# Routing ranks and loads reordered in the prologue, a ramp issued early, and MoE buffers placed above the attention output

## The chip, the cores and the metric

The kernel runs on one core of a Trainium2 chip. The metric is the device time of one execution in microseconds. Before the change it is 383.17 us, the median of 3 runs (382.03 to 384.43). The profiled execution has a span of 377.3 us; all times inside the kernel below are counted from the start of that span.

## The reference

The computation has two parts. The first is attention with a relative-position bias, for 8 batches, 8 heads, 576 positions and head size 64:

```
scores = q @ k^T / sqrt(64) + bias_table[bucket(|i - j|)]     per head
x      = softmax(scores) @ v            -> reshaped to [8*576, 512]
```

The bucket depends on the distance alone; distances of 128 and more share the last bucket. The second part is a mixture of experts (MoE) with a hashed choice: token t goes to expert `token_ids[t] * 2654435761 % 8`, and its row becomes `relu(x @ w1[e]) @ w2[e]`, with w1 of 512 x 1024 and w2 of 1024 x 512 for each of 8 experts. Since the multiplier is odd and ends in binary 001, the expert is the low three bits of the token's id.

## The kernel before

**Attention.** The 8 batches and 4 head pairs give 32 pairs, handled one after the other by a loop over n (0 to 31), with one more turn (n = 32) that finishes the last pair. For one pair:

- `load` and `load_v` bring q, k and v in; `cast_q` (L274) and `cast_k` (L283) on VectorE make 16-bit copies qh and kh; `cast_v` (L289) does so on ScalarE into vt.
- `transpose_q` and `transpose_k` transpose on TensorE (L457, L472) into a PSUM buffer of the tag aux, which has two buffers, and VectorE copies the result to qt (L465) and to kz (L478, L479). There are three kz; half of each is zero for good, written once by `z_init`.
- `scores(n, g)` for g = 0 to 3 multiplies into one of two PSUM buffers of the tag ps (L502), and ScalarE takes the exponential into att: three large ones (L513) and a tail (L507).
- `band` multiplies the exponentials near the diagonal by the exponential of the bias, ebd, on VectorE (L532). The last rows use ebd in two pieces for the first four pairs (L547), and later ebs, one piece (L552), which `make_ebs` copies from ebd. `low_bands` is the part of the bands that needs the tail.
- `av_steps(n)` is a generator: `advance(av, k)` issues the next k matmuls of att against v (L579) into two aux buffers in turn, with a reciprocal and a product (L589, L590) after each, which write the rows of x_all. It runs one pair behind: turn n holds the av of pair n - 1.

**Order.** [...] it is written out by hand. [...] Loads from HBM stand in SyncE's queue (`nc.sync`), some in ScalarE's and GpSimd's.

**Bias.** The table is loaded as tbl, turned by a small matmul (L712) and an exponential (L718) into one row per head, written to HBM (t_f, L722) and read back shifted by partition with `load_bias` (L727) into ebd.

**Routing.** `route` is a generator of twelve steps: te (low bits of the ids raw), tef (16-bit copy), ef (transposed by TensorE, L312), oh (one-hot), then the ranks inc and rnk (two matmuls into a ps buffer, L338 and L339, a scan and a subtraction), mx, flag and so on to the slot numbers ds2. Steps are taken in the prologue, at n = 0 and from n = 3 on. From n = 14 on, `name_slot` (L619) writes each token's row number to its slot in HBM by an indirect DMA from GpSimd; all slots are then loaded back as xid.

**The seam.** `store` (L634, L639) writes x_all to HBM. `gather(e, ...)` (L153) fetches five blocks of 128 rows for expert e by indirect DMAs from GpSimd; for expert 0 this happens at n = 30, when all batches but one are stored. The rows of the last batch that belong to expert 0's first block are fetched by a matmul with a one-hot matrix instead: `hot_slots` is a generator whose first step writes a ramp on GpSimd (L404) and a copy of the slots on VectorE (L408), and whose later steps make one matrix hot each (L414). `first_rows` (L424, L428) transposes blocks 1 to 4 inside turn 31, `first_slots` (L443, L448) makes block 0.

**MoE.** For each expert, 64 matmuls make hps (L953) in two PSUM buffers, ScalarE makes h from it (L959), 40 matmuls make ops (L977), VectorE copies them to ok (L984), and GpSimd scatters the rows to the output (L985). The pool of the MoE buffers (h1, xpt, ok) opens when attention's pool closes, and takes the same addresses: h1 lay where x_all had been.

Of the kernel before, what the change touches and what calls it, by code (L numbers as in the profile page):

```python
# [31 lines left out]
def kernel(  # L32
# [160 lines left out]
    with tc.tile_pool(name="at", bufs=1) as at, tc.tile_pool(  # L193
# [52 lines left out]

        def load_v(n):
            b, m = pairs[n]
            for hh in range(2):
                nc.sync.dma_start(  # L250
                    out=vf[n % 4][:, hh, :, :],
                    in_=v[b, 2 * m + hh, :NB4].rearrange(
                        "(t p) d -> p t d", p=P
                    ),
                )
# [262 lines left out]
        def band(n, g, lo=0):  # L518
# [20 lines left out]
            else:  # L539
                a = att[:, NU - 1, :QW].rearrange("p (o u) -> p o u", o=2)[  # L540
                    :, :, :EW
                ]
                if n < NPAIR:
                    for hh in range(2):
                        w0 = EW - HD * hh
                        r = slice(D * hh, D * hh + D)
                        nc.vector.tensor_tensor(  # L547
                            out=a[r], in0=a[r],
                            in1=ebd[r, :, m, hh, w0 : w0 + EW], op=ALU.mult,
                        )  # L550
                else:
                    nc.vector.tensor_tensor(  # L552
                        out=a, in0=a, in1=ebs[:, :, m, :], op=ALU.mult
                    )
# [88 lines left out]
        def advance(it, count):  # L643
            for _ in range(count):
                if next(it, "end") == "end":
                    return
# [11 lines left out]
        ohsb = at.tile([2 * NB, FW], F16, name="ohsb")  # L658
        nc.scalar.dma_start(out=ohsb[:, :], in_=OH_d.ap())
        nc.gpsimd.dma_start(out=ident[:, :], in_=I128_d.ap())  # L660
        load(0, "qk")
        load(1, "qk")

        def z_init(i):
            nc.vector.memset(kz[i][D:P, :S].bitcast(I32), 0)
            nc.vector.memset(kz[i][:D, S:].bitcast(I32), 0)

# [40 lines left out]
        z_init(1)  # L708
        z_init(2)
        FH = FW // 2  # L710
        for i in range(2):
# [11 lines left out]
            out=F_d.ap(), in_=ebsb[:, :, :].rearrange("h a b -> h (a b)")  # L723
        )
        def load_bias(eng, m0, m1, b2):
            for o in range(2):
# [11 lines left out]
        def make_ebs():  # L738
            for hh in range(2):
# [7 lines left out]
                )  # L747

        cast_q(0)
        cast_k(0)  # L750
        v_init(0)
        vs_init(0)
        for i in range(1, 4):
            v_init(i)
        nobody = at.tile([P, NSLOT // P, 2], I32, name="nobody")
        nc.gpsimd.memset(nobody[:, :, :], BIG)
        load_bias(nc.scalar, 0, 1, 0)
        load_bias(nc.sync, 0, 1, 1)
        load(0, "v")
        load(2, "qk")  # L760
        load_vs(0, nc.gpsimd)
        ids = moe_token_ids.bitcast(I32).rearrange(
            "(b s c) -> b s c", b=B, c=2
        )
        nc.gpsimd.dma_start(out=raw[:1, :, :], in_=ids[B - 1 :])
        nc.gpsimd.dma_start(out=raw[1:, :, :], in_=ids[: B - 1])
        nc.gpsimd.dma_start(out=msk[:, :], in_=MSK_d.ap())
        nc.gpsimd.dma_start(out=cnt[:, :], in_=CNT_d.ap())
        transpose_q(0)
        keep_busy(idp[:, :], 1)  # L770
        transpose_k(0)
        keep_busy(idp[:, :], 1)
        cast_q(1)
        cast_k(1)
        routing = route()
        advance(routing, 2)
        nc.gpsimd.tensor_copy(out=pace[:, :], in_=kh[1][:1, 0, 0, 0:1])
# [27 lines left out]
        for n in range(NP + 1):  # L805
# [11 lines left out]
            if n == 1:  # L817
                vs_init(1)
            if n == 3:
                make_ebs()  # L820
# [15 lines left out]
            for g in range(NSG + 1):  # L836
                scores(n, g)
                if 3 <= n < 14 and g == 1:
                    next(routing, None)
# [4 lines left out]
                if n == NP - 1:  # L844
                    for sc in ((), (1,), (2, 3), (4,))[g]:
                        first_rows(sc)
                if NP - 2 <= n and g in (0, 1, 3):
                    next(hotting, None)
                if n == 0:
                    if g == 1:  # L850
                        transpose_q(1)
                        transpose_k(1)
                        advance(routing, 2)
                        band(n, 0)
# [8 lines left out]
                elif n == 1:  # L863
# [4 lines left out]
                    elif g == 1:  # L868
                        advance(av, 27)
                        band(n, 0)  # L870
                    elif g == 2:
                        advance(av, 99)
                        band(n, 1)
                        band(n, 2)
                    elif g == 3:
                        transpose_k(2)
                        transpose_q(2)
                        cast_v(1)
# [5 lines left out]
                elif g == 0:  # L884
                    if n < NP - 1:
                        transpose_k(n + 1)
                    low_bands(n - 1)
                    advance(av, 12)
                elif g == 1:
                    if n == 2:  # L890
                        transpose_q(3)
                        cast_v(2)
                        load_v(6)
                        cast_q(4)
                    if n + 2 < NP:
                        cast_k(n + 2)
                    if 2 < n < NP - 1:
                        cast_v(n + 1)
                    advance(av, 15)
                    band(n, 0)  # L900
                elif g == 2:
                    if n < NP - 3:
                        cast_q(n + 3)
                    if n == 2:
                        cast_v(3)
                    advance(av, 99)
# [12 lines left out]
    with tc.tile_pool(name="mo", bufs=1) as mo, tc.tile_pool(  # L919
        name="mop", bufs=1, space=bass.MemoryType.PSUM  # L920
    ) as mop:
        NRC = 2
        NR = CAP // NRC
# [208 lines left out]
```

The softmax here doesn't subtract the row's maximum and nothing guards it: scores larger than these inputs give would overflow.

## Time and profile before

| engine | busy us | share of 377.3 us |
|---|---|---|
| TensorE matmul | 329.2 | 87% |
| ScalarE | 237.2 | 63% |
| VectorE | 218.7 | 58% |
| GpSimd | 186.3 | 49% |

| stretch, us | VectorE busy | ScalarE busy | TensorE matmul busy | granted TensorE clock |
|---|---|---|---|---|
| 8 to 20 | 9.67 | 9.26 | 9.79 | 1.00 |
| 20 to 30 | 8.28 | 5.23 | 7.20 | 0.83 |
| 140 to 160 | 19.04 | 17.92 | 17.67 | 1.00 |
| 190 to 200 | 4.68 | 6.45 | 9.61 | 0.72 |
| 200 to 210 | 2.98 | 4.36 | 3.17 | 0.79 |
| 210 to 222 | 7.96 | 3.55 | 9.96 | 0.89 |
| 242 to 260.5 | 3.52 | 8.51 | 18.50 | 1.00 |

A share of the whole span mixes three stages with different limits, so the second table is of more use: in steady attention (140 to 160) VectorE and ScalarE are both nearly full, in the MoE (242 to 260.5) TensorE alone is. Between 190 and 222 us no engine is full. Rows of one operation can overlap by about 0.1 us, so that a busy sum can come near the length of its stretch with short gaps left.

The tail exponentials (L507), one for each pair, are a clock of the attention's progress: pair 0 at 14.82, 1 at 20.05, 2 at 31.29, 3 at 38.36, 4 at 44.93, 13 at 98.37, 28 at 186.14, 29 at 195.89, 30 at 202.26, 31 at 216.18. The first full h of the MoE starts at 224.54.

### The profile page before, as it was taken

Reading aid. Unit: us, or ns where it says so; the run is one execution under the profiler, and the core shown is the slowest. Engines: PE = TensorE matmul, PEld = TensorE weight load, DVE = VectorE, ACT = ScalarE, POOL = GpSimd, SP = SyncE. Lnnn points to the kernel's source line nnn. Section 1 sums busy time; section 2 is a strip of 40 time slices with the busy share of each in tenths; the row PEclk is TensorE's granted clock in tenths of the full one; section 3 lists DMA queues with packets and bytes.
Section 4 is the critical chain, followed back from the end, with each engine's and each line's share of the span. In section 5 each row is a group of like instructions: output and inputs, shape, how many; then the busy total and the mean of one; then the engine's idle time right before and its main releaser. Section 6 shows DMA issues by size and latency. Waiting matters only on the chain.

```text
span 377.3 us, 8871 instructions
## 1 busy us (share of the span) xinstructions
PE 329.2 (87%) x3463; PEld 220.1 (58%) x3463; DVE 218.7 (58%) x593; ACT 237.2 (63%) x261; POOL 186.3 (49%) x304
## 2 busy tenths in 40 slices
PE   7868888898888988989784779999999999999991
PEld 2545665666666766666562556566665656565650
DVE  5889999999999999999941740212121212112121
ACT  2857888989988989889955315454544444444420
POOL 7801010221258848758425007588679677742322
PEclk9989999999999999999969799999999999999997
DMA  7899997998978999998841014849999999997212
GB/s 173 200 254 245 228 207 183 211 208 205 219 152 181 197 246 166 179 232 150 175 67 55 3 64 91 214 101 200 241 199 246 236 257 227 215 204 136 89 59 83
DMA packets 125525, 66.01 MB, mean 175 GB/s; under 512 B 86326, under 2 KB 117695, under 8 KB 125474
## 3 DMA queue, kind: packets, MB, share of 16 engines
q0 software_dynamic: 19744, 31.90, 41.3%
q1 hardware_dynamic: 105346, 33.25, 37.5%
q8 instruction: 29, 0.48, 0.5%
q10 hardware_dynamic: 384, 0.21, 0.2%
q14 instruction: 22, 0.18, 0.2%
HBM read 68.28 MB, written 15.30 MB: 222 GB/s over the span
## 4 chain that ended last, share of the span: by engine, by line
PE 52%; DVE 18%; DMA 9%; issue 7%; ACT 7%; POOL 4%; SPq 2%; POOLq 0%; ACTq 0%; DVEq 0%
PE ops L977 18%; PE hps L953 18%; PE ps L502 7%; DVE att L532 6%; PE px L579 5%; ACT att L513 4%; DVE x_all L590 4%; DMA t_x<-x_all 3%; ACT vt L289 2%; PE xps L930 2%; DMA t_id<-pay,ds 2%; DMA kf<-in_k_dram 2%; DVE qh L274 1%; DMA vf<-in_v_dram 1%; DVE rcp L589 1%
## 5 line engine op out<-in xcount | busy, mean ns | idle before, releaser
L513 ACT ACTIVATE att<-ps 128x1536 f16<-128x1536 f32 x96 | 138.6, 1448 | 40.5 <-PE ps L502 25.7
L502 PE MATMUL ps<-qt,kz 128*128 128x512 f16 (+1 forms) x576 | 94.9, 294 | 23.9 <-ACT att L513 21.2
L984 DVE COPY ok<-ops 128x512 f32<-128x512 f32 x40 | 27.7, 692 | 120.5 <-PE ops L977 109.6
L579 PEld LDWEIGHTS <-att 128*128 128x128 f16 x1440 | 76.7, 99 | 29.6 <-issue 10.6
L579 PE MATMUL px<-vt,att 128*128 128x98 f16 x1280 | 83.9, 210 | 7.8 <-DVE x_all L590 4.8
L977 PE MATMUL ops<-w2t,h 128*128 128x512 f16 x320 | 74.9, 379 | 0.0
L959 ACT ACTIVATE h<-hps 128x640 f16<-128x640 f32 x64 | 44.9, 704 | 42.8 <-PE hps L953 35.1
L532 DVE TENSOR_TENSOR att<-att,ebd 128x384 f16<-128x384 f16 (+2 forms) x192 | 70.0, 393 | 0.9
L953 PEld LDWEIGHTS <-w1t 128*128 128x128 f16 x512 | 50.1, 98 | 21.8 <-issue 1.4
L953 PE MATMUL hps<-xpt,w1t 128*128 128x320 f16 x448 | 62.0, 299 | 0.0
L985 POOL DMA_INDIRECT out_dram<-ok,xid x40 | 39.5, 988 | 45.1 <-DVE ok L984 35.1
L502 PEld LDWEIGHTS <-kz 128*128 128x128 f16 x576 | 37.2, 99 | 41.4 <-issue 25.8
L153 POOL DMA_INDIRECT xg<-t_x,xid x40 | 41.2, 1029 | 19.3 <-DMA t_x<-x_all 9.3
L977 PEld LDWEIGHTS <-h 128*128 128x128 f16 x320 | 30.1, 98 | 29.9
L619 POOL DMA_INDIRECT t_id<-pay,ds x40 | 41.8, 1044 | 8.8 <-issue 6.7
L934 ACT ACTIVATE xpt<-xps 128x512 f16<-128x512 f16 x35 | 20.1, 596 | 37.1 <-PE xps L930 37.1
L579 PE MATMUL px<-vs,att 128*128 128x132 f16 x160 | 36.1, 226 | 2.3 <-POOL vs L267 1.8
L590 DVE TENSOR_TENSOR x_all<-px,rcp 128x384 f16<-128x384 f32 x64 | 31.4, 491 | 2.4 <-DVE rcp L589 0.2
L603 POOL COPY pace<-rcp 1x1 f32<-1x1 f32 x39 | 9.1, 233 | 42.9 <-DVE rcp L589 42.7
L267 POOL CAST vs<-vsf 64x256 f16<-64x256 f32 x16 | 7.5, 471 | 45.5 <-DMA vsf<-in_v_dram 27.7
L507 ACT ACTIVATE att<-ps 128x576 f16<-128x576 f32 x32 | 20.8, 651 | 1.1 <-PE ps L502 1.1
L289 ACT ACTIVATE vt<-vf 128x512 f16<-128x512 f32 x32 | 19.9, 623 | 0.1
(84 smaller groups left out, 266.5 us busy)
## 6 DMA issues: line engine op xcount, KB each, us to landing
qf<-in_q_dram SPq DMA_DIRECT2D x32, 288.0 KB
kf<-in_k_dram SPq DMA_DIRECT2D x32, 288.0 KB, 4.5
vf<-in_v_dram SPq DMA_DIRECT2D x64, 128.0 KB, 5.2
w1t<-in_moe_w_dram POOLq DMA_DIRECT2D x6, 1024.0 KB, 10.8
w2t<-in_moe_w_dram POOLq DMA_DIRECT2D x6, 1024.0 KB
t_x<-x_all SPq DMA_DIRECT2D x7, 512.0 KB
w1t<-in_moe_w_dram POOLq DMA_DIRECT2D x8, 256.0 KB
w2t<-in_moe_w_dram POOLq DMA_DIRECT2D x8, 256.0 KB, 7.2
```

The costliest lines, as they stand in the source:

```text
L153: nc.gpsimd.indirect_dma_start(out=xg[e % 3][:, sc, :], out_offset=None, in_=x_d.ap()[: S * nb, :], in_offset=bass.IndirectOffsetOnAxis(ap ...
L502: nc.tensor.matmul(out=out_ap, lhsT=z[:, k0 : k0 + P], rhs=rhs, start=True, stop=True,)
L513: nc.scalar.activation(out=att[:, 3 * g : 3 * g + 3, :QW], in_=ps[:, :, :], func=AF.Exp, bias=0.0, scale=scale,)
L532: nc.vector.tensor_tensor(out=a, in0=a, in1=ebd[:, :, m, :, a0 + w0 : a1 + w0].transpose([0, 2, 1, 3]), op=ALU.mult,)
L579: nc.tensor.matmul(out=px[:, ii, o : o + w], lhsT=lhsT, rhs=rhs, start=(y == 0), stop=(y == len(todo) - 1), skip_group_check=True,)
L590: nc.vector.tensor_tensor(out=x_all[:, b, its[0] : its[0] + ni, P * m : P * m + P].rearrange("p t (h d) -> p t h d", h=2), in0=pv[:, :, :, ...
L619: i = nc.gpsimd.indirect_dma_start(out=id_d.ap()[:, :], out_offset=bass.IndirectOffsetOnAxis(ap=ds2[:, g : g + 1], axis=0), in_=pay[:, g, ...
L953: nc.tensor.matmul(out=hps[:, nr, :NR], lhsT=w1h[:, kt, ts(ft, P)], rhs=xt[e][:, kt, ts(nr, NR)], start=(kt == 0), stop=(kt == NPT - 1),)
L959: nc.scalar.activation(out=h1[:, ft, :].rearrange("p (r n) -> p r n", r=NRC), in_=hps[:, :, :NR], func=AF.Relu, bias=0.0, scale=1.0,)
L977: nc.tensor.matmul(out=ops[:, :], lhsT=h1[:, ft, ts(kc, P)], rhs=w2h[:, ft, :], start=(ft == 0), stop=(ft == NFT - 1),)
L984: nc.vector.tensor_copy(out=ok[:, :], in_=ops[:, :])
L985: so = nc.gpsimd.indirect_dma_start(out=out[:, :], out_offset=bass.IndirectOffsetOnAxis(ap=xid[:, NSC * e + kc, 1:2], axis=0), in_=ok[:, : ...
```

## The change

It does these things:

- In the prologue, the ids (raw) are loaded from ScalarE's queue and the two tables that routing needs (msk, cnt) from GpSimd's, all at the very start, and the first five routing steps, the ranks among them, are taken in the prologue. Before, two were taken there, two at n = 0 and the ranks at n = 3; the later steps now run at n = 5 to 13.
- ScalarE writes one element of pair 1's kf buffer from ebsb after the bias table's write is issued. This makes the load of pair 1's k, and the loads of pair 2 behind it in the queue, start after that write. Pair 2's q and k stood behind the bias loads and pair 0's v before.
- The kz buffer of pair 2 is zeroed by GpSimd, and two warm-up matmuls of the prologue (`keep_busy`) go.
- The transposes of pairs 2 and 3 stand at other places of turns 1 and 2; `make_ebs` runs at n = 2, and pair 3 already uses ebs.
- The first step of `hot_slots` (ramp and slot copy) is taken at n = 16; the five later ones each move one place forward.
- A tile of the size of x_all, never used, is put first in the MoE pool, so that h1, xpt and ok lie above x_all's addresses.

The parameter `eng` of `load_v` is not used by any call.

```diff
--- before.py
+++ after.py
@@ -244,10 +244,10 @@
             if what == "qkv":
                 load_v(n)
 
-        def load_v(n):
+        def load_v(n, eng=nc.sync):
             b, m = pairs[n]
             for hh in range(2):
-                nc.sync.dma_start(
+                eng.dma_start(
                     out=vf[n % 4][:, hh, :, :],
                     in_=v[b, 2 * m + hh, :NB4].rearrange(
                         "(t p) d -> p t d", p=P
@@ -540,7 +540,7 @@
                 a = att[:, NU - 1, :QW].rearrange("p (o u) -> p o u", o=2)[
                     :, :, :EW
                 ]
-                if n < NPAIR:
+                if n < 3:
                     for hh in range(2):
                         w0 = EW - HD * hh
                         r = slice(D * hh, D * hh + D)
@@ -657,13 +657,20 @@
         )
         ohsb = at.tile([2 * NB, FW], F16, name="ohsb")
         nc.scalar.dma_start(out=ohsb[:, :], in_=OH_d.ap())
+        ids = moe_token_ids.bitcast(I32).rearrange(
+            "(b s c) -> b s c", b=B, c=2
+        )
+        nc.scalar.dma_start(out=raw[:1, :, :], in_=ids[B - 1 :])
+        nc.scalar.dma_start(out=raw[1:, :, :], in_=ids[: B - 1])
         nc.gpsimd.dma_start(out=ident[:, :], in_=I128_d.ap())
+        nc.gpsimd.dma_start(out=msk[:, :], in_=MSK_d.ap())
+        nc.gpsimd.dma_start(out=cnt[:, :], in_=CNT_d.ap())
         load(0, "qk")
-        load(1, "qk")
-
-        def z_init(i):
-            nc.vector.memset(kz[i][D:P, :S].bitcast(I32), 0)
-            nc.vector.memset(kz[i][:D, S:].bitcast(I32), 0)
+        load(1, "q")
+
+        def z_init(i, eng=nc.vector):
+            eng.memset(kz[i][D:P, :S].bitcast(I32), 0)
+            eng.memset(kz[i][:D, S:].bitcast(I32), 0)
 
         idle = at.tile([P, 512], F16, name="idle")
         nc.vector.memset(idle[:, :].bitcast(I32), 0)
@@ -706,7 +713,6 @@
                 )
 
         z_init(1)
-        z_init(2)
         FH = FW // 2
         for i in range(2):
             nc.tensor.matmul(
@@ -722,6 +728,13 @@
         nc.scalar.dma_start(
             out=F_d.ap(), in_=ebsb[:, :, :].rearrange("h a b -> h (a b)")
         )
+        nc.scalar.activation(
+            out=kf[1][:1, 0, 0, 0:1], in_=ebsb[:1, 0, 0:1], func=AF.Copy,
+            bias=0.0, scale=1.0,
+        )
+        load(1, "k")
+        load(2, "qk")
+
         def load_bias(eng, m0, m1, b2):
             for o in range(2):
                 eng.dma_start(
@@ -746,34 +759,28 @@
                     ),
                 )
 
+        routing = route()
+        advance(routing, 1)
         cast_q(0)
+        advance(routing, 1)
         cast_k(0)
+        load_bias(nc.scalar, 0, 1, 0)
+        load_bias(nc.sync, 0, 1, 1)
+        transpose_q(0)
+        advance(routing, 2)
         v_init(0)
         vs_init(0)
+        transpose_k(0)
+        advance(routing, 1)
+        load_vs(0, nc.gpsimd)
+        z_init(2, nc.gpsimd)
         for i in range(1, 4):
             v_init(i)
         nobody = at.tile([P, NSLOT // P, 2], I32, name="nobody")
         nc.gpsimd.memset(nobody[:, :, :], BIG)
-        load_bias(nc.scalar, 0, 1, 0)
-        load_bias(nc.sync, 0, 1, 1)
-        load(0, "v")
-        load(2, "qk")
-        load_vs(0, nc.gpsimd)
-        ids = moe_token_ids.bitcast(I32).rearrange(
-            "(b s c) -> b s c", b=B, c=2
-        )
-        nc.gpsimd.dma_start(out=raw[:1, :, :], in_=ids[B - 1 :])
-        nc.gpsimd.dma_start(out=raw[1:, :, :], in_=ids[: B - 1])
-        nc.gpsimd.dma_start(out=msk[:, :], in_=MSK_d.ap())
-        nc.gpsimd.dma_start(out=cnt[:, :], in_=CNT_d.ap())
-        transpose_q(0)
-        keep_busy(idp[:, :], 1)
-        transpose_k(0)
-        keep_busy(idp[:, :], 1)
+        load_v(0)
         cast_q(1)
         cast_k(1)
-        routing = route()
-        advance(routing, 2)
         nc.gpsimd.tensor_copy(out=pace[:, :], in_=kh[1][:1, 0, 0, 0:1])
         for b2 in range(2):
             load_bias(nc.gpsimd, 1, 2, b2)
@@ -816,7 +823,7 @@
             b, m = pairs[n]
             if n == 1:
                 vs_init(1)
-            if n == 3:
+            if n == 2:
                 make_ebs()
             if b + 1 < B and m == 1:
                 load_vs(b + 1)
@@ -835,7 +842,7 @@
                 (load_w1 if w == 1 else load_w2)(e, y, y + w)
             for g in range(NSG + 1):
                 scores(n, g)
-                if 3 <= n < 14 and g == 1:
+                if 5 <= n < 14 and g == 1:
                     next(routing, None)
                 if n == NP - 3 and g == 1:
                     store(B - 2, 0, NIT)
@@ -844,13 +851,12 @@
                 if n == NP - 1:
                     for sc in ((), (1,), (2, 3), (4,))[g]:
                         first_rows(sc)
-                if NP - 2 <= n and g in (0, 1, 3):
+                if n == 16 and g == 0 or NP - 2 <= n and g in (0, 1, 3):
                     next(hotting, None)
                 if n == 0:
                     if g == 1:
                         transpose_q(1)
                         transpose_k(1)
-                        advance(routing, 2)
                         band(n, 0)
                     elif g == 2:
                         band(n, 1)
@@ -869,12 +875,12 @@
                         advance(av, 27)
                         band(n, 0)
                     elif g == 2:
+                        transpose_k(2)
+                        transpose_q(2)
                         advance(av, 99)
                         band(n, 1)
                         band(n, 2)
                     elif g == 3:
-                        transpose_k(2)
-                        transpose_q(2)
                         cast_v(1)
                         load_v(5)
                         band(n, 3)
@@ -882,27 +888,31 @@
                         cast_k(3)
                         cast_q(3)
                 elif g == 0:
-                    if n < NP - 1:
+                    if 2 < n < NP - 1:
                         transpose_k(n + 1)
                     low_bands(n - 1)
                     advance(av, 12)
                 elif g == 1:
                     if n == 2:
-                        transpose_q(3)
                         cast_v(2)
                         load_v(6)
+                        advance(av, 15)
+                        transpose_k(3)
                         cast_q(4)
                     if n + 2 < NP:
                         cast_k(n + 2)
                     if 2 < n < NP - 1:
                         cast_v(n + 1)
-                    advance(av, 15)
+                    if n > 2:
+                        advance(av, 15)
                     band(n, 0)
                 elif g == 2:
+                    if n == 2:
+                        cast_v(3)
+                        advance(av, 99)
+                        transpose_q(3)
                     if n < NP - 3:
                         cast_q(n + 3)
-                    if n == 2:
-                        cast_v(3)
                     advance(av, 99)
                     band(n, 1)
                     band(n, 2)
@@ -919,6 +929,7 @@
     with tc.tile_pool(name="mo", bufs=1) as mo, tc.tile_pool(
         name="mop", bufs=1, space=bass.MemoryType.PSUM
     ) as mop:
+        mo.tile([P, B * NIT * DM], F16, name="above")
         NRC = 2
         NR = CAP // NRC
         NSC = CAP // P
```

## The prediction

> **What bounds the kernel now.** I read the page's slices first: TensorE is busy at eight tenths through the attention, dips in slices 20 to 22 (188 to 217 us), and is at nine and more afterwards. So there are three stretches: attention up to 188 us, a seam, and a MoE part that is TensorE alone.
>
> ```profile
> PE   7868888898888988989784779999999999999991
> PEclk9989999999999999999969799999999999999997
> ```
>
> Then the table of waits. Most of its long entries belong to engines that are not the bound (VectorE waits 109.6 us for the MoE's matmuls, which costs nothing). Three single waits of over 4 us stand in the seam:
>
> ```profile
> DVE hot L414 <- POOL ramp L404: 7.7, 1, 7.7
> ACT h L959 <- DMA t_x<-x_all: 7.7, 1, 7.7
> PE px L579 <- DVE x_all L590: 4.8, 1, 4.8
> ```
>
> The timeline of 199 to 213 us shows how they hang together; columns are start, duration, engine, line, operation, and in brackets the idle time before it.
>
> ```profile
> 200.22 1.05 POOL L153 DMA_INDIRECT xg<-t_x,xid  x1 [9.30 <-DMA t_x<-x_all]
> ...
> 205.52 1.01 POOL L153 DMA_INDIRECT xg<-t_x,xid  x1 [0.30 <-issue]
> 206.62 0.26 POOL L404 IOTA ramp<- 128x128 f16 x1
> 206.92 0.25 DVE L414 TENSOR_SCALAR hot<-ramp,slot 128x128 f16<-128x128 f16 x1 [7.67 <-POOL ramp L404]
> ...
> 208.05 0.32 PE L579 MATMUL px<-vt,att 128*128 128x98 f16 x2 [4.82 <-DVE x_all L590]
> ...
> 212.32 1.45 ACT L513 ACTIVATE att<-ps 128x1536 f16<-128x1536 f32 x1 [7.55 <-PE ps L502]
> ```
>
> GpSimd's ramp stands behind five gathers, these behind the store of x, and VectorE waits 7.67 us for the ramp with ready work behind it; TensorE and ScalarE then run dry. Between two ScalarE tail exponentials (L507) lie 5.75 us in steady state, but 13.92 us here.
>
> At the start, VectorE is the bound: from 9.3 to 45 us its rows follow each other with three gaps, 0.27, 1.36 and 1.40 us.
>
> ```profile
> 18.06 0.56 DVE L283 CAST kh<-kf 96x768 f16<-96x768 f32 x1 [1.36 <-DMA kf<-in_k_dram]
> ...
> 23.10 0.82 PE L502 MATMUL ps<-qt,kz 128*128 128x512 f16 x3 [1.78 <-DVE qt L465]
> ...
> 24.01 1.45 ACT L513 ACTIVATE att<-ps 128x1536 f16<-128x1536 f32 x1 [2.78 <-issue]
> ...
> 27.74 0.46 DVE L465 COPY qt<-pq 128x576 f16<-128x576 f16 x1 [1.40 <-PE pq L457]
> ```
>
> Pair 2's k is issued at 12.33 because SyncE waits 4.0 us for the bias table's write in front of it; its landing holds VectorE.
>
> [...] the granted mean is 0.79 in 200 to 210 us and 1.00 in 140 to 160. [...] the gathers in the seam land in 2.8 us, the x store in 2.0, but loads at the busy start in 4.1 to 4.9. [...] the trace has one table load in all, though copies and exponentials alternate.
>
> **The change, part by part.**
>
> *Ramp and slot copy at pair 16.* Removes the 7.67 us wait. Following each engine without it: hot 0 runs at 199.3; the reciprocal that ran at 207.21 needs matmuls done at 199.8; x_all, bands and hot 1 and 2 then take VectorE to 203.6; the nine matmuls of pair 30 that need the last band run to 204.1, scores of pair 31's second group to 204.9 (0.81), so the exponential that started at 212.32 starts at 204.9: 7.4 us. Next limit, the gathers: row block 3 is issued at 204.21, block 4 at 205.52; with 2.8 us they land at 207.0 and 208.3. The transposes of blocks 2 and 3 then start at 207.3 (0.3 of it is from the next paragraph), the second half of the attention's av follows (0.8), scores (0.45), and block 4's transposes run at 209.2 in place of 215.98. Gain 6.8 us (bounds: 7.4 if nothing waits for a gather; 2.4 if gathers take the page's median 7.8 us and block 4 lands at 213.6).
>
> The ramp now stands in GpSimd's queue at pair 16. From 102 us to 191 us GpSimd is back to back (slot naming, pace copies, memsets), and at 189.59 TensorE waits 1.84 us for its cast of vs. So 0.26 plus a start gap, 0.3 us, is paid in full: -0.3.
>
> *MoE buffers above x_all.* Removes the wait of the first h for the last store:
>
> ```profile
> 222.29 2.33 PE L953 MATMUL hps<-xt,w1t 128*128 128x320 f16 x16 [0.38 <-DVE xt L448]
> ...
> 224.54 1.30 ACT L959 ACTIVATE h<-hps 128x640 f16<-128x640 f32 x2 [7.71 <-DMA t_x<-x_all]
> 225.30 6.68 PE L953 MATMUL hps<-xt,w1t 128*128 128x320 f16 x48 [0.68 <-ACT h L959]
> ```
>
> Not 7.7 us: the first hps is complete at about 223.45, h could start there, and TensorE, which has two hps buffers, stands still only 0.68 us. Gain 0.7 (0.3 to 1.0). The regions now written (kz, ebd, qf, kf) have had their last reader before. The gathers for expert 1 move forward too and have 5 us of slack.
>
> *Prologue.* VectorE work that leaves the stretch after 9.3 us: te and tef (10.28 to 11.56, net 1.2), ef and oh (0.67): 1.9 us; the gap of 0.27 beside them; the kf gap 1.36, since pair 2's q and k are issued at about 6.5 to 7.5 and with 4.1 to 4.5 us land near 11.5; the pq gap 1.40, since pair 2's and 3's transposes stand elsewhere; 0.26 because pair 3 uses the one-piece bias (0.25 for 0.51). Gross 5.2 us. The ranks (0.82 + 0.49) only move. Zeroing kz 2 on GpSimd takes 0.7 us from VectorE when it waits for q anyway (0.51 idle at 5.58); on GpSimd, scaled from a 128x424 memset at 0.47, it costs 0.7 before 8 us, needed at 19. [...] The ebs copies one pair earlier are 1.3 us of SyncE queue, hidden behind loads already issued.
>
> Against it stand new waits:
> - te ahead of the first cast of q, behind it on VectorE q, tef, k, and so TensorE's first scores. The ids are issued on ScalarE at 1.3 and 1.85; the trace shows small loads at 2.4 to 3.5 us, so about 4.5 to 5.4, te until 5.2 to 6.1, first kz 0.25 later.
> - The rank matmuls take a ps buffer, so pair 0's second scores wait for the rank subtraction, and pair 1's transposes and exponentials behind them: VectorE idle 0.7.
> - GpSimd's pace copy follows the k cast of pair 1, at 12.0 in place of 10.43. Behind it: pair 1's bias (last issue at 14.5, landing with 4.4 at 18.9; band needed at 18.5: 0.4) and the vs cast (16.3, needed at 16.9).
> - Pair 2's transposes take both aux buffers, so the second half of pair 0's av, with the fourth scores behind it, waits for kz 2: the tail exponential at 21.7 for 20.05; VectorE idle 0.55.
> - VectorE waiting for av at pairs 0, 2 and 3: 0.15 + 0.75 + 0.6.
>
> Sum 3.4; net gain 5.2 - 3.4 = 1.8 us by pair 4. Bounds: 3.5 if half of the new idle is absent, -0.5 if ids and pair 1's bias each come 1 us later. ScalarE's floor, 5.75 us a pair from pair 0's tail (14.8), would allow 7 us, so it does not cap this. The routing steps from mx on move by a pair or two: nothing. SyncE's k of pair 1 waits for ScalarE's copy (about 5.9): behind it pair 2's loads; it is needed at 11.4 and lands near 10.3.
>
> Between pairs 4 and 29 nothing changes; the gain carries through, since GpSimd's chain starts with pair 13's output and moves with it. MoE steady state (18.44 us an expert) stays.
>
> Sum: 6.8 - 0.3 + 0.7 + 1.8 = 9.0; 383.17 - 9.0 = 374.2.
>
> **The rivals.**
> 1. *Gathers take the ramp's place*: landing 7.8 us as in the page, block 4 at 213.6. [...] Against: DMA is nearly idle there, 2.8 us. 2.4 - 0.3 + 0.7 + 1.8 = 4.6: 378.6.
> 2. *The prologue gives more*: the new idle mostly closes up because loads and table write land earlier (SyncE's 4 us hole, in which the DMA engines are at five tenths or less from 7.8 to 12 us, is filled). Prologue 4.5, ramp 7.2: 12.1, 371.1. Against: av and transposes share two aux buffers.
> 3. *Slower*: ids take 6.3 us (the slowest small transfer) and land at 8.2: te 3.3 later than q; the held-back av costs 1.3 in pairs 1 and 2 each; pair 1's bias 0.4; the gathers bind (2.4). 3.3 + 2.6 + 0.4 - 2.4 - 0.7 = +3.2: 386.4. Against: raw was ready within 3.5 us before, under heavier load.
>
> **How the numbers follow.** Main 0.62, rival 1 0.15, rival 2 0.18, rival 3 0.05. The time is the main case's. The range goes from rival 2 less a run's scatter of 1.1 us (370.0) to rival 1 (378.6). One per cent is 379.3: rival 1's upper edge crosses it a little, so faster 0.92, same 0.05, slower 0.03.
>
> **What would show it.** Ramp: no VectorE wait on L404, tail-exponential distance of pair 31 near 7 us for 13.92, granted clock near 1 in the seam; a wait of TensorE for a gather at the row transposes means rival 1. Placement: no h wait on the store, first expert shorter by 0.7. Prologue: pair 2's k cast without DMA wait, the tail exponential of pair 4 at about 43.1 for 44.93; above 45 the prologue step is wrong. GpSimd: TensorE's vs wait near 2 us; if it grows, the 0.3 was too small. The prediction fails most easily in the prologue, where five small new waits were placed by hand.

## The result and the profile after

The changed kernel takes 370.94 us (median of 4 runs, 367.79 to 371.71); the kernel before, run beside it, 382.60 us (4 runs, 381.38 to 384.43). The ratio is 0.9676, with a 95% interval of 0.9606 to 0.9745: 11.7 us less, where 9.0 were forecast. The two profiled executions are closer to each other, 377.3 and 369.1 us of span, because the profiled execution of the kernel before (379.21 us) was quicker than all its timed ones. What follows explains those 8.2 us; the other 3.5 us have no trace. Here and below, ratios and their intervals leave out executions that took over 1.5% longer than the quickest of the same kernel in the same comparison, and profiles of such executions are not compared.

The slices of the page after:

```profile
PE   6777898888989888878877789999999999999991
PEclk9998999999999999999999999999999999999996
```

The hole in slices 20 to 22 is shallower, and the granted clock no longer falls there. The table of waits (us in total, number, longest) shows what stands in the seam now:

```profile
POOL xg L153 <- DMA t_x<-x_all: 8.5, 1, 8.5
ACT h L970 <- DMA t_x<-x_all: 6.8, 1, 6.8
PEld L424 <- DMA xg<-t_x,xid: 3.6, 2, 2.7
PE xr L424 <- DMA xg<-t_x,xid: 3.0, 2, 2.2
PE px L579 <- POOL vs L267: 2.6, 2, 1.4
DVE te L299 <- DMA raw<-in_moe_token_ids_dram: 1.3, 1, 1.3
```

VectorE's 7.7 us for the ramp are gone. New are two waits of TensorE for gathers, 3.0 us together. The first h still waits for a store, though its buffer lies elsewhere. The timeline of the seam:

```profile
200.18 1.15 POOL L153 DMA_INDIRECT xg<-t_x,xid  x1 [8.47 <-DMA t_x<-x_all]
200.31 0.25 DVE L414 TENSOR_SCALAR hot<-ramp,slot 128x128 f16<-128x128 f16 x1
201.63 1.02 POOL L153 DMA_INDIRECT xg<-t_x,xid  x1 [0.30 <-issue]
...
204.41 0.40 PE L424 MATMUL xr<-ident,xg 128*128 128x128 f16 x4 [2.21 <-DMA xg<-t_x,xid]
...
207.11 0.40 PE L424 MATMUL xr<-ident,xg 128*128 128x128 f16 x4 [0.76 <-DMA xg<-t_x,xid]
...
214.08 2.33 PE L964 MATMUL hps<-xt,w1t 128*128 128x320 f16 x16 [0.38 <-DVE xt L448]
216.09 1.30 ACT L970 ACTIVATE h<-hps 128x640 f16<-128x640 f32 x2 [6.83 <-DMA t_x<-x_all]
216.85 6.68 PE L964 MATMUL hps<-xt,w1t 128*128 128x320 f16 x48 [0.44 <-ACT h L970]
```

The gathers are issued at the same times as before (200.18 for 200.22), yet VectorE makes its third hot matrix while the first gather is being issued, where before it made the first one at 206.92, and the MoE's first matmul starts at 214.08 for 222.29. So the seam now ends by attention's own work and the gathers, not by the ramp behind them.

The clock of tail exponentials (L507) tells where the 8.21 us before that first matmul come from:

| stretch | before | after | gain |
|---|---|---|---|
| start to pair 4 | 44.93 | 44.51 | 0.42 |
| pair 4 to 14 | 59.19 | 58.91 | 0.28 |
| pair 14 to 28 | 82.02 | 83.76 | -1.74 |
| pair 28 to 29 | 9.75 | 7.08 | 2.67 |
| pair 29 to 30 | 6.37 | 5.69 | 0.68 |
| pair 30 to 31 | 13.92 | 8.67 | 5.25 |
| pair 31 to the first hps | 6.11 | 5.46 | 0.65 |
| first hps to the end | 155.01 | 155.02 | 0.0 |

The row of pair 29 had not been foreseen. In the kernel before, TensorE waits there 1.84 us for the cast of vs and then works slowly (timeline, TensorE alone):

```profile
189.59 0.27 PE L579 MATMUL px<-vs,att 128*128 128x132 f16 x1 [1.84 <-POOL vs L267]
...
191.70 0.86 PE L579 MATMUL px<-vt,att 128*128 128x98 f16 x8
```

The same place after the change:

```profile
190.03 0.22 PE L579 MATMUL px<-vs,att 128*128 128x132 f16 x1 [1.23 <-POOL vs L267]
...
191.14 0.51 PE L579 MATMUL px<-vt,att 128*128 128x98 f16 x8
```

Eight matmuls take 0.86 us in place of 0.51. Cut by the microsecond, the trace of before has a granted clock (last but two of the numbers) of one half:

```profile
191.00:192.00 1.00, 1.00 (x11) 0.81 (x10) 0.00 (x0) 0.57 (x1) 0.00 (x0) 0.50 0.03 1
```

It is 0.50 from 188.8 to 195.6 us there, and 1.00 from 180 to 222 us after the change. The low clock begins inside the wait of 1.84 us, which ends at 189.59; over the longer wait of 2.21 us after the change, which ends at 204.41, the clock stays at 1.00. So the length of the wait alone does not tell the two apart, and what lowered the clock is not shown. No other profile took over 7.1 us for that pair: this part of the gain belongs to the one profiled execution of before and not surely to the change.

### The profile page after: what moved, and what is told of

Same layout as the page of the kernel before. It is cut to its first block, busy times and chain, and to the rows that moved or that the text cites. A ratio compares the mean times of both kernels' runs of the same rounds, so it can differ in the third digit from the quotient of the medians.

```text
span 369.1 us, 8870 instructions
## 1 busy us (share of the span) xinstructions
PE 323.6 (88%) x3461; PEld 216.9 (59%) x3461; DVE 219.1 (59%) x590; ACT 236.8 (64%) x262; POOL 188.3 (51%) x304
## 4 chain that ended last, share of the span: by engine, by line
PE 49%; DVE 16%; DMA 14%; issue 7%; POOL 6%; ACT 5%; SPq 1%; POOLq 0%; ACTq 0%; DVEq 0%
PE ops L988 19%; PE hps L964 18%; DVE att L532 6%; PE px L579 4%; PE ps L502 4%; DMA vf<-in_v_dram 3%; DMA t_id<-pay,ds 3%; DVE x_all L590 3%; ACT att L513 3%; POOL t_id L619 2%; DMA t_x<-x_all 2%; PE xps L941 2%; ACT vt L289 2%; DMA ebd<-t_f 1%; DVE rcp L589 1%
## 5 line engine op out<-in xcount | busy, mean ns | idle before, releaser
L502 PE MATMUL ps<-qt,kz 128*128 128x512 f16 (+1 forms) x576 | 92.3, 288 | 22.4 <-ACT att L513 21.2
L579 PEld LDWEIGHTS <-att 128*128 128x128 f16 x1440 | 74.9, 98 | 25.3 <-issue 5.7
L579 PE MATMUL px<-vt,att 128*128 128x98 f16 x1280 | 81.4, 207 | 3.2 <-DVE kz L479 1.4
L502 PEld LDWEIGHTS <-kz 128*128 128x128 f16 x576 | 36.2, 98 | 39.2 <-issue 25.8
L507 ACT ACTIVATE att<-ps 128x576 f16<-128x576 f32 x32 | 20.9, 653 | 2.7 <-PE ps L502 2.7
```

The lines of the kernel that those rows point to most:

```text
L502: nc.tensor.matmul(out=out_ap, lhsT=z[:, k0 : k0 + P], rhs=rhs, start=True, stop=True,)
L579: nc.tensor.matmul(out=px[:, ii, o : o + w], lhsT=lhsT, rhs=rhs, start=(y == 0), stop=(y == len(todo) - 1), skip_group_check=True,)
```

## Experiments

They ran in three later comparisons, on two chips. In all three the kernel before took about 390 us (medians 390.61, 390.26, 389.41), 2% more than in the first comparison. Ratios are against runs of the kernel before in the same comparison.

### The ramp alone

```diff
-                if NP - 2 <= n and g in (0, 1, 3):
+                if n == 16 and g == 0 or NP - 2 <= n and g in (0, 1, 3):
```

> The kernel before, with the ramp and slot copy taken at pair 16 alone. My theory: this part carries nearly all of the gain. The VectorE wait on the ramp (7.67 us) is gone; the gathers now end TensorE's waits in turn 31 (about 3 us in all), so the distance of the last two tail exponentials falls from 13.9 to 8 to 9 us, and the time by 5 to 8 us against before. Rival (the prologue carries part of it): 3 to 4 us only, with the gathers taking the ramp's place.

> The ramp edit alone, once more, beside the changed kernel. My theory: on a fast chip it carries 5 to 8 us of the 8 to 12; on a slow one 1 to 2 us. Rival (together only): 1 to 2 us also where the whole change gains 8 or more.

> The kernel before with only the ramp and the slot naming moved to pair 16. Where the kernel before reaches pair 30 at about 202 us and VectorE waits there some 7 us for the ramp (time near 382), my theory gives 5 to 7 us less for this edit alone: 375 to 377, and pairs 30 and 31 under 9 us apart. Where the kernel before takes about 390 and reaches pair 30 at about 215, it gives 0 to 1.5 us, as in the two runs before. The rival, that the ramp carries little and the gain of the whole change comes from elsewhere, gives 0 to 1.5 us in both.

The edit is the same in all three: it moves the ramp and the slot copy, and the slot naming stays where it was. Measured: 0.9962 (0.9934 to 0.9990), 0.9971 (0.9945 to 0.9998), 1.0003 (0.9969 to 1.0037), that is -1.5, -1.1 and +0.1 us. The 6.8 us of the forecast are not there. Why, is seen best in the kernel before itself, run once more.

### The kernel before and the kernel after once more

> The kernel before, unchanged, for a second profile of it on the same chip as the runs beside it. Open question: on the chip of the part-by-part runs the kernel before took 390.6 us and the ramp part gained 0.4 per cent only. My theory: whether VectorE waits for the ramp depends on how far attention runs ahead of GpSimd's slot naming; where transfers delay attention between pairs 14 and 28, the wait on the ramp is near zero and the ramp edit has nothing to remove. So where the tail exponential of pair 28 comes at 186 us, a ramp wait of 5 us or more; where it comes at 200, under 2 us. Rival: the ramp wait is there on every chip and the edit brings in another wait.

> The changed kernel, unchanged, on the same chip. My theory: if this chip is a slow one (before near 390), its gain is the prologue's 0.5 to 1 us and the ramp's 1 to 2, so 1 to 3 us; if it is a fast one (before near 382), 8 to 12 us as first measured. Rival (the parts work only together): 8 us or more on either chip.

> The whole change once more, beside its parts on one chip. My theory: 8 to 12 us less than the kernel before where that takes about 382, 5 to 7 us less where it takes about 390. If the parts add up, the whole lies within 1.5 us of the sum of the two part runs beside it; the rival, that the parts work only together, has the whole over 2 us below that sum.

Measured: the kernel before 0.9995 (0.9964 to 1.0025). The kernel after 0.9850 (0.9814 to 0.9886), and 0.9971 (0.9938 to 1.0005) in the last comparison: 5.9 and 1.1 us less, where 5 to 7 were expected of the last. The 5.9 us rest on 8 of the 20 executions of the changed kernel (381.84 to 387.11 us); by the medians of all executions it takes 388.42 us there and the kernel before 390.26, 1.8 us more. The gain of 11.7 us did not come again. The seam of the kernel before in its repetition (from the timeline):

```profile
206.56 1.07 POOL L153 DMA_INDIRECT xg<-t_x,xid  x1 [7.92 <-DMA t_x<-x_all]
...
211.88 1.01 POOL L153 DMA_INDIRECT xg<-t_x,xid  x1 [0.30 <-issue]
213.00 0.26 POOL L404 IOTA ramp<- 128x128 f16 x1
213.29 0.26 DVE L414 TENSOR_SCALAR hot<-ramp,slot 128x128 f16<-128x128 f16 x1 [4.35 <-issue]
```

The bracket says "issue", but hot starts 0.03 us after the ramp's end: it is the same wait, 4.35 us in place of 7.67. Under 2 us had been expected, so the wait is shorter, but it does not go. In the first profile attention passes pair 28 at 186.14, 14.1 us ahead of the first gather; here at 200.37, 6.2 us ahead. GpSimd's chain had fallen back by 6.3 us, attention by 14.2. Pair 29 with its slow clock costs the first profile 3.9 us of that lead. At pair 29's tail the lead is 4.33 us there and 0.30 us here, and -0.33, -0.69 and -0.70 us in the other three profiles with the old ramp; their waits for the ramp are 7.67, 4.35, 3.92, 3.33 and 3.32 us. The less attention leads, the shorter it waits, by some 0.8 us for each microsecond from the first profile to the second. No run moves the lead alone, so this is a comparison of five profiles and not a proof.

Without that wait, another stands at the same place. The kernel with the ramp alone, third run:

```profile
208.78 1.01 POOL L153 DMA_INDIRECT xg<-t_x,xid  x1 [0.30 <-issue]
210.10 1.00 POOL L153 DMA_INDIRECT xg<-t_x,xid  x1 [0.30 <-issue]
211.08 0.20 DVE L589 RECIPROCAL rcp<-px 128x6 f32<-128x6 f32 x1 [3.06 <-PE px L579]
```

VectorE is idle for 3.06 us. Over the later profiles that are compared: the four kernels with the old ramp lose 3.3 to 4.4 us (mean 3.7) on hot, the five with the new one 2.5 to 3.1 us (mean 2.75) on this reciprocal. From pair 29 to 31 they take 15.2 to 16.3 us (mean 16.0) and 14.6 to 15.5 us (mean 15.3); in the first comparison it was 20.3 and 14.4. From there to the first hps every kernel with the old ramp takes 6.11 us and every one with the new 5.46. So under these conditions the edit is worth some 1.4 us, near two of the three times (1.5 and 1.1 us, and none in the third). What holds the reciprocal no run settles. It needs the first 27 matmuls (px), and by its row the last of these had ended at 208.18, 2.9 us before; ends of matmuls are modelled, but the row names TensorE as what ended the wait, at 211.08. In two of the five profiles VectorE goes on just as the last gather's issue ends (211.10 here), in three others 0.25 to 0.32 us after that issue begins. So the rival named with the kernel before, that taking the first wait away brings in another, is in part what was found.

### Where the later runs lose their time

All later kernels keep the pace of the first comparison up to pair 14 (58.9 to 59.3 us for pairs 4 to 14) and then need 94 to 99 us for pairs 14 to 28, where the first comparison needed 82.0 and 83.8. Most of the loss stands at pairs 15 to 18, 20 to 22 and 24 to 27. The MoE takes longer too, 157.8 to 158.9 us for 155.0. In the two profiles of the kernel before, 9.05 us apart, pairs 14 to 28 make 13.7 us more, pairs 28 to 31 7.9 us less and the MoE 2.75 us more. The repeated changed kernel of the last comparison (timeline, then stretches of 2 us, with the granted clock last but two):

```profile
115.85 0.81 PE L502 MATMUL ps<-qt,kz 128*128 128x512 f16 x3 [0.54 <-issue]
...
117.46 0.74 PE L472 MATMUL pk<-ident,kh 96*128 96x96 f16 x7 [0.80 <-DVE x_all L590]
...
120.23 0.81 PE L579 MATMUL px<-vt,att 128*128 128x98 f16 x8 [2.03 <-DVE qt L465]
```

```profile
114.00:116.00 2.00, 0.58 (x7) 0.42 (x8) 1.49 (x4) 1.45 (x1) 1.82 (x5) 1.00 1.16 273
116.00:118.00 2.00, 1.20 (x10) 0.64 (x9) 1.21 (x4) 0.00 (x0) 1.70 (x4) 0.75 0.68 138
118.00:120.00 2.00, 0.20 (x3) 0.06 (x1) 0.55 (x2) 0.83 (x2) 1.83 (x4) 0.50 0.41 85
120.00:122.00 2.00, 1.77 (x14) 1.26 (x14) 1.96 (x8) 1.27 (x1) 0.19 (x1) 0.50 0.80 167
```

First TensorE, VectorE and ScalarE stall with little that the profile can name; then, at 117.0 us, after two microseconds (114 to 116) with 0.58 us of TensorE's work, the granted clock falls from 1.00 to 0.50 until 123.8, and the pair's work takes longer still. So a lower clock follows the stalls here and does not begin them. GpSimd is at work up to about 120.2 us (1.82 us of 2 at first), issuing the slot writes that start with pair 14, and then waits 4.20 us itself for a reciprocal. The loss begins with these writes in all later profiles, but no cause is shown: the first comparison has the same writes without the loss. That transfers as a whole are slower is not shown either: the packets in pairs 14 to 28 take 76.9 to 81.7 us of the 16 DMA engines in the later profiles, and 77.5 and 74.8 us in the first two. Single late transfers are not ruled out.

### The prologue alone

The changed kernel with the old condition for the ramp and without the tile above:

```diff
-                if n == 16 and g == 0 or NP - 2 <= n and g in (0, 1, 3):
+                if NP - 2 <= n and g in (0, 1, 3):
...
-        mo.tile([P, B * NIT * DM], F16, name="above")
```

> The prologue edits alone: ramp and MoE buffers as before. My theory: the tail exponential of pair 0 comes 1.3 us later than before, that of pair 4 about 0.4 earlier, and the 7.7 us wait on the ramp stays, so the time is within 1.5 us of before. Rival (the prologue is worth the 1.8 us of the prediction, or more): pair 4 at about 43.1 and the time 2 us or more below before.

> The prologue's part alone (routing steps early, pair 2's loads behind the bias table's write), the ramp where it was. My theory, after the profiles: 0.4 to 0.7 us ahead at pair 4, and where VectorE waits for the ramp at pair 31 that lead is lost in the wait unless the slot naming also comes earlier: 0 to 2 us less than the kernel before. The rival, that the prologue carries most of the whole change, gives 6 us or more.

Measured: 0.9947 (0.9918 to 0.9977) and 0.9963 (0.9920 to 1.0005): 2.1 and 1.4 us less. Pair 4's tail stands at 43.47 to 45.56 us in the five profiles with the new prologue and the early ranks (mean 44.46), and at 44.93 to 46.27 in five with the old one (mean 45.63). At pair 14 the means are 103.56 and 104.82. So the prologue gives about 1.2 us, and a single pair of profiles, with 2 us of spread, can't tell that from 0.4 or from 1.8. The first of the two runs decides for neither theory: pair 0's tail is at 17.84, 3.0 us later than in the kernel before and not 1.3, pair 4's at 45.56, 0.6 later and not earlier, and yet the time is 2.1 us less.

### The routing steps back in their old places

```diff
-        routing = route()
-        advance(routing, 1)
         cast_q(0)
-        advance(routing, 1)
         cast_k(0)
...
+        routing = route()
+        advance(routing, 2)
...
-                if 5 <= n < 14 and g == 1:
+                if 3 <= n < 14 and g == 1:
```

> The changed kernel with the routing steps back in their old places (two after pair 1's casts, two in turn 0, the rest from turn 3 on); everything else as changed. My theory: the steps in front of the first casts cost about 1.5 us at pair 0 (waiting for the ids, and 16-bit copies slowed beside GpSimd's memsets), so the first tail exponential falls from 16.1 to about 14.6, pair 4 to 43 to 44, and the time is 0 to 1.5 us below the changed kernel. Rival (VectorE is the bound and the ranks only come back at pair 3): pair 0 gains, pair 4 does not, and the time is the changed kernel's or 1 us above it.

Measured: 0.9914 (0.9878 to 0.9951), 387.64 us; pair 4's tail at 44.14, pair 14's at 103.14, within the spread of the early ranks. Pair 0's tail was to fall from 16.14 to about 14.6 and stands at 16.13. (The slower copy that was expected to matter is tef: 1.05 us beside GpSimd's memsets after the change, 0.45 in the kernel before.) Another wait has taken the place of the routing steps:

```profile
6.67 0.86 DVE L274 CAST qh<-qf 96x768 f16<-96x768 f32 x1 [2.12 <-DMA qf<-in_q_dram]
...
9.32 0.45 DVE L478 COPY kz<-pk 64x576 f16<-64x576 f16 x1 [0.47 <-PE pk L472]
```

The load of q is issued at 1.50 us as in the kernel before, where the cast of q waits 0.51 us for it; it comes 1.1 us later, with the small loads of routing now beside it at the very start; no run takes these away alone. First kz is at 9.32, for 8.36 before and 10.08 after the change. So 0.96 of the 1.72 us by which the change delays it stay without the early steps. The first exponential then starts at 12.02, behind ScalarE's issue of the bias loads (10.68, for 8.94 before). One profile can't tell less than a microsecond at pair 4, but the early ranks are not what the prologue's gain hangs on: the order of loads and transposes, which this kernel keeps, gives about as much without them.

### The tile above alone

```diff
+        mo.tile([P, B * NIT * DM], F16, name="above")
```

> The unused tile above the attention output alone. My theory: the first h waits for the release of the whole attention pool, the last store among it, wherever it lies; TensorE's wait for the first h stays at 0.4 to 0.7 us and the time is that of before within noise. Rival (h waited for the store because it lay where x_all had been): no wait of TensorE there, and the first h about 1.2 us after the first hps matmul instead of 2.0 to 2.3.

Measured: 1.0018 (0.9993 to 1.0044), nothing. The page of waits has the same line as before the change:

```profile
ACT h L960 <- DMA t_x<-x_all: 7.7, 1, 7.7
```

In the built program x_all lies at bytes 71,680 to 112,640 of a partition and h1 at 112,640, just above, as the change means it. Yet the wait stays. Two theories were open: the wait is for the release of the whole attention pool, whatever bytes are written, or it is something of ScalarE's order.

### The first h in memory outside that pool's release

The changed kernel with the first two tiles of h for expert 0 in a gather buffer that has been read by then:

```diff
+            early = xg[2][:, :, :].rearrange("p s d -> p (s d)")[
+                :, : 2 * CAP
+            ].rearrange("p (f n) -> p f n", f=2)
+
+            def hv(ft):
+                return early[:, ft, :] if e == 0 and ft < 2 else h1[:, ft, :]
```

> The changed kernel with the first two activation tiles of expert 0 written into a gather buffer that has been read by then, so that the first activation needs no memory of the attention pool. If the first activation waits for the release of that pool as a whole, its 6.8 us wait for the stores is gone here, TensorE's wait for h of 0.44 us falls to under 0.1, and the kernel gains 0.3 to 0.8 us on the changed one. If the wait belongs to the engine's order or to the output itself, it stays and the time is the same.

Measured, in the timeline:

```profile
225.90 8.86 PE L971 MATMUL hps<-xt,w1t 128*128 128x320 f16 x64 [0.38 <-DVE xt L448]
...
227.32 0.70 ACT L977 ACTIVATE xg<-hps 128x640 f16<-128x640 f32 x1 [6.23 <-PE hps L971]
```

ScalarE's first h is now released by its own matmuls, and TensorE runs all 64 matmuls without the stop of 0.46 us that the changed kernel beside it has. This settles it for the first theory: the wait belonged to the pool's release. As for time, 384.10 us (4 runs, ratio 0.9842, 0.9780 to 0.9905) is the best of the last comparison, under the changed kernel's 0.9971. But the part that the edit touches, first hps to the end, is 158.6 us for 158.5: the difference lies in attention, whose code is the same. The mechanism is shown, the 0.3 to 0.8 us expected of it are not.

### Blanking the gather buffers sooner

The 30 memsets that zero the gather buffers stand one at a time between the slot writes on GpSimd. Three are taken at once here, so that they are done sooner:

```diff
-                    if blank:
-                        i, j = blank.pop(0)
+                    for i, j in [blank.pop(0) for _ in range(min(3, len(blank)))]:
```

> The changed kernel, with GpSimd's 30 memsets of the gather buffers taken three to an av half from pair 7 on, so that they end before the slot naming starts. My theory: GpSimd's chain of slot naming, xid and gathers ends the seam, so 18 memsets less in it (0.25 us each) bring xid and the gathers 4 us earlier; TensorE's waits for row blocks 1 and 3 (2.2 and 0.8 us) and for the vs cast (1.2) go, and the time falls 2 to 4 us below the changed kernel. Rival (attention, not GpSimd, sets the seam): the gathers come 4 us earlier and the time stays within 1 us.

Measured: 0.9925 (0.9880 to 0.9970), where the changed kernel of the same comparison has 0.9850: the 2 to 4 us expected below the changed kernel are not there. No trace of it is read here, so whether the gathers came sooner, and what GpSimd's memsets cost, stays open.

## Why the prediction was right, and where it was not

The time, 370.9, lies within the range of 370.0 to 378.6 and 3.3 us under the forecast. Step by step:

- **Ramp, 6.8 us.** Right. From pair 29 to the first hps the gain is 0.68 + 5.25 + 0.65 = 6.6 us, and the wait is gone. Rival 1 asked for gathers that land after 7.8 us: they land about 2.8 us after their issue (201.63 to 204.41). They do take over as the last limit, but at block 1 as well as at block 3: TensorE waits 2.21 us at 204.41, where the working began with blocks 2 and 3. With these waits (2.21 and 0.76 us) pair 31's tail comes 8.67 us after pair 30's, where near 7 was to show.
- **What the ramp step left out** is that its size rests on attention's lead over GpSimd's chain, taken from one trace as if it were a property of the kernel. With 4.3 us of lead at pair 29's tail the edit gives 6.6 us, with 0.3 us and less about 1.4.
- **Ramp in GpSimd's queue, -0.3 us.** The wait for vs at pair 29 was to stay near 2 us; it is 1.23. GpSimd runs 0.79 us later there (last slot write at 190.72 for 189.93), but the first gather starts at the same time. It waits for the store, and the store stands in SyncE's queue behind the load of xid, which needs the slot writes. In the kernel before

```profile
192.07 0.37 SPq L829 DMA_DIRECT2D xid<-t_id  x1
...
195.26 0.51 SPq L639 DMA_DIRECT2D t_x<-x_all  x1
```

and after the change

```profile
193.07 0.37 SPq L836 DMA_DIRECT2D xid<-t_id  x1
...
196.67 0.51 SPq L639 DMA_DIRECT2D t_x<-x_all  x1
```

  So the delay reached the store, 1.4 us by its last part, and the gathers start together only because the store landed sooner after its issue this time (the first gather follows that issue by 3.51 us, by 4.96 before). The -0.3 us is neither shown nor refuted. The rows of this store were complete at 185.8 and 186.8 us, some 7 us before its first part was issued; whether a store put ahead of xid would start the gathers sooner, no run tried.
- **Tile above, 0.7 us.** Wrong: 0.0. The step that failed is "removes the wait of the first h for the last store". The overlap of h1 with x_all was read as the cause of the wait; the cause is the release of the pool. That TensorE would lose only its own stop, and not 7.7 us, was right: that stop is 0.44 us now.
- **Prologue, 1.8 us.** Right in sign and mis-sized: 0.4 us by pair 4 in the pair of profiles, about 1.2 over ten. The term that failed is "first kz 0.25 later": it is 1.72 later (10.08 for 8.36). The load of q, whose delay was put at nothing, came about 1 us later beside the new small loads: with the routing steps back, 0.96 us of the delay stay. The ids came a little late (te starts at 6.08, with 1.34 us of waiting), and VectorE's work beside GpSimd's memsets took longer than its old rows say. In the timeline of before the cast tef is

```profile
11.11 0.45 DVE L308 CAST tef<-te 8x576 f16<-8x576 int32 x1
```

and after the change

```profile
7.40 1.05 DVE L308 CAST tef<-te 8x576 f16<-8x576 int32 x1
8.38 0.53 DVE L283 CAST kh<-kf 96x768 f16<-96x768 f32 x1
...
10.08 0.45 DVE L478 COPY kz<-pk 64x576 f16<-64x576 f16 x1
```

  Pair 2's k came without a wait, as said (its cast is at 17.87), and pair 2's tail stands 1.38 us earlier than before.
- **"Between pairs 4 and 29 nothing changes"** holds to pair 14 (0.28 us). Pairs 14 to 28 then lose 1.74 us, 1.45 of it at pair 25 (7.40 us for 5.95), one of the places where all later runs stall, and pair 29 gains 2.67, where the granted clock is 1.00 and not 0.50. Neither was in the sum; together they are +0.9.

The sum of what was measured, 0.42 + 0.28 - 1.74 + 2.67 + 6.58 + 0.0 = 8.2 us, is near the 9.0 of the forecast partly because 0.9 us of pairs 14 to 29 make up for some of what the tile (0.7) and the prologue (1.4 by pair 4) did not bring. The 11.7 us of the timed runs contain 3.5 us that the forecast did not have. The forecast's range is 4.6 to 13.2 us less: the first comparison lies in it, and so do the 5.9 us of the second later one, but not the 1.1 us of the last, nor the 1.8 and 1.5 us between the medians of all executions of those two. So the forecast was right on its main step under the conditions of the trace that it was worked from; that the conditions came once more in the first comparison was luck, and the number is luckier than its parts deserve.

No run shows that the parts work only together. In the last comparison the whole gives 1.1 us and the parts -0.1 + 1.4. The 5.9 us of the one before are more than ramp and prologue gave in the first later one (1.5 + 2.1), but by medians of all executions the whole gives 1.8 and 1.5 us, the ramp 0.4 to 1.1 and the prologue 1.3 and 2.2.

Left open: why the runs of the first comparison were 2% quicker than all later ones; what stalls pairs 15 to 27; what lowers the granted clock at 188.8 us in the kernel before; and what delays TensorE's event beside the gathers.

## What to carry to other kernels

What the removal of a wait between two chains gives grew here with the lead of the chain that waits: before pricing it, measure how far that chain is ahead and what stands next at the same place, and expect the price to change when anything earlier slows that chain. A buffer moved to free addresses gained nothing here, since its pool opened on the release of another (the wait of 7.7 us stayed); look at what the wait is for in the trace after the smallest such edit. One profile is one execution: compare the steps over several profiles of kernels that share them before a difference of 1 us is believed.

## What the runs showed of the hardware

In the traces before and after the change small VectorE operations took longer beside GpSimd memsets: tef 1.05 us after the change (7.40 to 8.45, memsets from 6.16 to 9.34) for 0.45 before (11.11, no memset beside it), te 0.92 for 0.73. Two memsets of kz on GpSimd, of one shape, took 0.38 and 1.16 us. No run isolates the cause.

While hot waited in the kernel before, VectorE ran nothing else: 0.01 us of its work lies in the 7.67 us up to 206.92, and the reciprocal whose matmuls had ended at 199.7 ran at 207.21. ScalarE's new one-element copy took 0.20 us (5.98) and brought no second table load: the traces before and after have one each, of 1.28 us. With two matmuls fewer in the prologue the granted clock was 1.00 from 0 to 20 us as before.

The granted clock was 0.50 from 188.8 to 195.6 us in the kernel before, where eight matmuls took 0.86 us for 0.51; it began inside a TensorE wait of 1.84 us, and stayed at 1.00 over one of 2.21 us after the change. The first activation written into the MoE's pool waited for a store of x_all, though it wrote to other addresses (6.8 us after the change, 7.7 with the tile alone), and did not where it wrote into an older buffer (released at 227.32 by its own matmuls, which began at 225.90). A gather of 128 rows reached its reader 2.8 us after its issue began (201.63 to 204.41), with 1.0 us of issue on GpSimd and 0.3 us between two. And one program had a median of 382.6 us in one comparison and 389.4 to 390.6 in three others, on two chips; between its two profiles, pairs 14 to 28 grew by 13.7 us and the MoE by 2.75, and pairs 28 to 31 shrank by 7.9.
